# A Mamba-2 scan followed by hash-routed experts: the scan's decays split into a factor per step, its units halved, and expert weights held five at a time

## The chip, the cores and the metric

The kernel runs on one core of a Trainium2 chip. The metric is device time in microseconds (us) of one execution. TensorE (PE; PEld is its weight load), VectorE (DVE), ScalarE (ACT), GpSimd (POOL) and the queue engine SyncE (SP) each work through their own instructions in order and wait for each other on semaphores.

## The reference

First a state-space scan, for 4 batches x 8 heads over 768 steps, with head size D = 32 and state size N = 16. Each step has a decay a in 0.85 to 0.95. It is written in chunks of steps:

```python
cum = np.cumsum(la, axis=-1)                      # la = log(a), inside the chunk
L = np.exp(cum[:, :, :, None] - cum[:, :, None, :]) * causal
M = np.einsum('bhin,bhjn->bhij', Cc, Bc) * L
y = M @ xc + (Cc @ state) * np.exp(cum)[..., None]
state = exp(sum(la)) * state + sum_j B_j x_j * exp(cum[-1] - cum_j)
```

Then y, as 3072 tokens of 256 values, goes through one of 8 experts each, `relu(x @ w1[e]) @ w2[e]`, with e = token_id mod 8, w1 256 x 1024 and w2 1024 x 256, all in float32. The expert of the inputs with the most tokens has 403.

## The kernel before

**Scan.** 24 chunks of 128 steps (4 batches x 6), all 8 heads in one chunk. `prepare(b)` (L283) brings B and C of a batch into the layout states x steps: B and C are copied (`rows`, L293 and L295), transposed on PE (L299), written out as `bt` (L301) and `ce` (L307, L309: C with the odd or the even head of each pair set to zero), and B is transposed back and multiplied by its decays (`bs`, L315). `chunk` (L321) makes, for each half of the heads: `rl`, the log decays on a triangle (L334 on ACT, L336 on DVE); `seg`, their sums over steps, by a bf16 mask product (L338) and a float32 product of 512 columns (L340); `dl`, its exponential (L342); `gram`, C times B (L347, 32 rows of the array, 256 columns); `m`, their product (L349); and y (L353, 128 rows and columns, 32 columns streamed, one product per head). Then the carried state enters: `sp` (L360), its product with C (L364), the decays and the sum (L366, L369), a write to `y_tokens` in HBM (L370), and the new state from `bs` and x (L376) on DVE (L382).

**Routing.** `routing()` (L194, after chunk 1) turns token ids into a slot for each token, on DVE with three small matmuls; `slot_token` (L269) writes 128 slot numbers at a time to HBM from POOL; after the last one `idx_out` is loaded (L276, SP) and `idx_in` is made of it (L277, DVE). It holds the rows that each expert gathers.

**Experts.** Eight experts, up to 416 tokens each. Rows are gathered by POOL (L418), transposed (L441), multiplied (L454 up, L464 down, 128 x 128 weights and 416 columns), transposed back (L478) and scattered (L423). The loop for tokens over 416 (L513) has no round with these inputs. Weights of all 8 experts (16 MB) lie on chip; `load_w` (L102) issues them on ScalarE's queue, two loads of 1 MB per expert, from chunk 0 on, one expert every second chunk.

A scheduler orders the instructions of each engine from the program's text and its own costs, so the order on an engine is not the order of the text. Float32 matmuls are issued as two passes: the trace shows two MATMUL for each.

Of the kernel before, what the change touches and what calls it, by code (L numbers as in the profile page):

```python
# [20 lines left out]
def kernel(  # L21
# [97 lines left out]
    after = const.tile([P, P], F32)  # L119
    nc.vector.tensor_scalar(out=after, in0=upto, scalar1=-1.0, scalar2=1.0, op0=OP.mult, op1=OP.add)  # L120
    low = const.tile([P, P], BF16)
    nc.vector.tensor_scalar(out=low, in0=upto, scalar1=1000.0, scalar2=-1000.0, op0=OP.mult, op1=OP.add)  # L122

    gmask = const.tile([P, G, 2 * D], F32)
    nc.gpsimd.memset(gmask, 1.0)
    nc.gpsimd.affine_select(out=gmask, in_=gmask, pattern=[[-32, G], [0, 2 * D]], compare_op=OP.is_ge,
                            fill=0.0, base=0, channel_multiplier=1)
    nc.gpsimd.affine_select(out=gmask, in_=gmask, pattern=[[32, G], [0, 2 * D]], compare_op=OP.is_ge,
                            fill=0.0, base=31, channel_multiplier=-1)
# [13 lines left out]
    la_ps = ps_t.tile([P, R, BH], F32, name="tp")
    for c in range(R):
        nc.tensor.transpose(out=la_ps[:, c], in_=la[:, c * P:(c + 1) * P], identity=ident[0:BH, 0:BH])
    laT = const.tile([P, R, BH], F32)
    nc.vector.tensor_copy(out=laT, in_=la_ps)
    laf = laT.rearrange("p c j -> p (c j)")

    dec_ps = ps_t.tile([P, 2, R, BH], F32, name="tp")  # L150
    decf = dec_ps.rearrange("p i c j -> p i (c j)")
    nc.tensor.matmul(out=decf[:, 0], lhsT=upto, rhs=laf, start=True, stop=True)
    nc.tensor.matmul(out=decf[:, 1], lhsT=after, rhs=laf, start=True, stop=True)
# [11 lines left out]
    mhn = apre.tile([BH, H, NS], F32)
    nc.vector.tensor_copy(out=mhn, in_=mh.unsqueeze(2).to_broadcast([BH, H, NS]))
    totb = apre.tile([BH, NB, R], F32)
    nc.vector.tensor_tensor(out=totb, in0=tot.unsqueeze(1).to_broadcast([BH, NB, R]),
                            in1=mb.unsqueeze(2).to_broadcast([BH, NB, R]), op=OP.mult)
    pend_ps = ps_t.tile([P, NCH], F32, name="tp")  # L170
# [403 lines left out]
```

## Time and profile before

| | before |
|---|---|
| median of 3 runs | 471.72 us (470.3 to 471.89) |
| the profiled execution | 472.49 us, span 470.5, mean granted clock 0.862 |
| PE / PEld busy | 402.8 / 237.5 us |
| DVE / ACT / POOL busy | 150.8 / 94.8 / 93.3 us |
| moved by DMA | 33.28 MB, 57,868 packets |
| chain that ended last | PE 50%, issue 24%, DMA 16% |

Busy time is an engine's own; a busy PE is not PE at its peak, since its instructions' ends are modelled and overlap. The granted clock is 1.0 at 2.4 GHz and 0.5 at 1.2 GHz. In the timeline, `x8` is eight instructions merged in one row; what such a row costs its engine is the distance to the start of the next row. The bracket at the end of a row is the idle time before it and what ended it.

### The profile page before, as it was taken

Reading aid. Unit: us, or ns where it says so; the run is one execution under the profiler, and the core shown is the slowest. Engines: PE = TensorE matmul, PEld = TensorE weight load, DVE = VectorE, ACT = ScalarE, POOL = GpSimd, SP = SyncE. Lnnn points to the kernel's source line nnn. Section 1 sums busy time; section 2 is a strip of 40 time slices with the busy share of each in tenths; the row PEclk is TensorE's granted clock in tenths of the full one; section 3 lists DMA queues with packets and bytes.
Section 4 is the critical chain, followed back from the end, with each engine's and each line's share of the span. In section 5 each row is a group of like instructions: output and inputs, shape, how many; then the busy total and the mean of one; then the engine's idle time right before and its main releaser. Section 6 shows DMA issues by size and latency. Waiting matters only on the chain.

```text
span 470.5 us, 4814 instructions
## 1 busy us (share of the span) xinstructions
PE 402.8 (86%) x1689; PEld 237.5 (50%) x1690; DVE 150.8 (32%) x401; ACT 94.8 (20%) x217; POOL 93.3 (20%) x108
## 2 busy tenths in 40 slices
PE   0689988960699999999983999999999999999960
PEld 0347564620455666666661555555555555555530
DVE  2354853200223655765631121212121212122120
ACT  2151231120012344333320102011111111111110
POOL 1100174420000000000005430505050512020221
PEclk9996995555555899999995899999999999999985
DMA  8966729875233322210002110202020100000000
GB/s 296 230 199 201 225 31 134 124 98 110 23 111 114 111 48 45 46 34 25 23 22 66 55 33 3 66 4 68 3 66 6 55 15 33 0 35 0 26 32 13
DMA packets 57868, 33.28 MB, mean 71 GB/s; under 512 B 42799, under 2 KB 54089, under 8 KB 57844
## 3 DMA queue, kind: packets, MB, share of 16 engines
q10 hardware_dynamic: 10496, 16.78, 13.6%
q1 hardware_dynamic: 43764, 9.62, 10.4%
q0 software_dynamic: 3584, 6.57, 4.5%
q8 instruction: 14, 0.23, 0.2%
q14 instruction: 10, 0.08, 0.1%
HBM read 26.63 MB, written 6.59 MB: 71 GB/s over the span
## 4 chain that ended last, share of the span: by engine, by line
PE 50%; issue 24%; DMA 16%; POOL 5%; DVE 2%; ACT 1%; SPq 0%; POOLq 0%; DVEq 0%
PE h_ps L454 12%; PE o_ps L464 11%; PE y_ps L353 7%; PE seg L340 7%; DMA slot_tokens<-token,slot_i 5%; PE gram L347 5%; DMA out_dram<-o_sb,idx_out 4%; DMA bc<-in_C_dram 4%; POOL slot_tokens L270 2%; PE seg L338 2%; POOL out_dram L423 2%; PE y_ps L364 2%; DMA idx_out<-slot_tokens 2%; PE xt_ps L441 1%; PE tp L376 1%
## 5 line engine op out<-in xcount | busy, mean ns | idle before, releaser
L464 PE MATMUL o_ps<-hT,w_sb 128*128 128x416 f32 x256 | 102.1, 518 | 0.0
L454 PE MATMUL h_ps<-xT,w_sb 128*128 128x416 f32 x256 | 101.7, 522 | 0.3 <-DVE xT L442 0.3
L353 PEld LDWEIGHTS y_ps<-x_t,m 128*128 128x128 f32 x384 | 60.3, 231 | 21.6 <-issue 10.1
L464 PEld LDWEIGHTS o_ps<-hT,w_sb 128*128 128x128 f32 x256 | 47.5, 190 | 40.1 <-issue 36.3
L454 PEld LDWEIGHTS h_ps<-xT,w_sb 128*128 128x128 f32 x256 | 47.1, 194 | 32.2 <-issue 30.6
L340 PE MATMUL seg<-rl,after 128*128 128x512 f32 x96 | 62.0, 733 | 0.4 <-ACT rl L334 0.4
L353 PE MATMUL y_ps<-x_t,m 128*128 128x32 f32 x384 | 59.2, 303 | 0.9 <-DVE m L349 0.9
L418 POOL DMA_INDIRECT xg<-y_tokens,idx_in x32 | 32.0, 1001 | 122.1 <-issue 92.0
L342 ACT ACTIVATE dl<-seg 128x512 f32<-128x512 f32 x48 | 28.5, 599 | 128.5 <-PE seg L340 118.1
L423 POOL DMA_INDIRECT out_dram<-o_sb,idx_out x32 | 31.3, 977 | 114.1 <-ACT o_sb L481 95.8
L347 PE MATMUL gram<-ce,bt 32*128 32x256 f32 x192 | 48.0, 492 | 0.0
L448 DVE TENSOR_SCALAR hT<-h_ps 128x416 f32<-128x416 f32 x32 | 18.9, 592 | 74.4 <-PE h_ps L454 74.4
L349 DVE TENSOR_TENSOR m<-gram,dl 128x512 f32<-128x512 f32 x48 | 32.8, 687 | 28.5 <-PE gram L347 20.9
L446 ACT ACTIVATE hT<-h_ps 128x416 f32<-128x416 f32 x32 | 16.5, 517 | 99.9 <-PE h_ps L454 81.4
L442 DVE COPY xT<-xt_ps 128x256 f32<-128x256 f32 (+1 forms) x32 | 12.0, 375 | 70.8 <-PE xt_ps L441 70.0
L270 POOL DMA_INDIRECT slot_tokens<-token,slot_i x24 | 23.9, 996 | 48.2 <-DVE slot_i L259 28.2
L334 ACT ACTIVATE rl<-upto,laT 128x128 f32<-128x128 f32 x96 | 31.8, 390 | 0.0
L338 PE MATMUL seg<-low,ident 128*128 128x512 bf16 x48 | 20.9, 448 | 12.3 <-DVE low L122 10.9
L347 PEld LDWEIGHTS gram<-ce,bt 32*128 32x128 f32 x192 | 20.1, 211 | 19.8 <-issue 16.0
L336 DVE TENSOR_SCALAR rl<-upto,laT 128x128 f32<-128x128 f32 x96 | 23.7, 284 | 16.8 <-PE seg L340 13.2
L376 PE MATMUL tp<-x_t,bs 128*32 128x64 f32 x160 | 8.1, 260 | 20.0 <-DVE s_new L382 20.0
L340 PEld LDWEIGHTS seg<-rl,after 128*128 128x128 f32 x96 | 19.8, 230 | 5.4 <-issue 2.6
(109 smaller groups left out, 216.3 us busy)
## 6 DMA issues: line engine op xcount, KB each, us to landing
w_sb<-in_moe_w_dram ACTq DMA_DIRECT2D x16, 1024.0 KB
x_t<-in_x_dram SPq DMA_DIRECT2D x24, 128.0 KB
y_tokens<-y_sb SPq DMA_DIRECT2D x24, 128.0 KB
bc<-in_B_dram SPq DMA_DIRECT2D x4, 384.0 KB
bc<-in_C_dram SPq DMA_DIRECT2D x4, 384.0 KB
xg<-y_tokens,idx_in POOLq DMA_INDIRECT x32
out_dram<-o_sb,idx_out POOLq DMA_INDIRECT x32
slot_tokens<-token,slot_i POOLq DMA_INDIRECT x24
```

What stands on the lines that cost most here:

```text
L270: st = nc.gpsimd.indirect_dma_start(out=slot_dram[:, None], out_offset=bass.IndirectOffsetOnAxis(ap=slot_i[:, c:c + 1], axis=0), in_=token ...
L334: nc.scalar.activation(rl[:, k], upto, AF.Copy, scale=w)
L338: nc.tensor.matmul(out=seg, lhsT=ident16, rhs=low.unsqueeze(1).to_broadcast([P, HH, P]), start=True, stop=False)
L340: nc.tensor.matmul(out=seg, lhsT=after, rhs=rl, start=False, stop=True)
L342: nc.scalar.activation(dl, seg, AF.Exp)
L347: nc.tensor.matmul(out=gram[:, k, 0:2 * P], lhsT=bt[r, t], rhs=ce[r, :, t], start=True, stop=True)
L349: nc.vector.tensor_tensor(out=m.rearrange("p (k e) i -> p k (e i)", k=2), in0=gram[:, :, 0:2 * P], in1=dl.rearrange("p (k e) i -> p k (e i ...
L353: nc.tensor.matmul(out=y_ps[:, 0, h0 + k], lhsT=m[:, k], rhs=x_t[:, h0 + k], start=True, stop=True)
L418: nc.gpsimd.indirect_dma_start(out=dst, out_offset=None, in_=y_dram[:], in_offset=bass.IndirectOffsetOnAxis(ap=idx, axis=0), bounds_check= ...
L423: st = nc.gpsimd.indirect_dma_start(out=out[:], out_offset=bass.IndirectOffsetOnAxis(ap=idx, axis=0), in_=src, in_offset=None, bounds_chec ...
L454: nc.tensor.matmul(out=hp, lhsT=w1_sb[:, c:c + P], rhs=xT[e][:, i], start=(i == 0), stop=(i == DP - 1))
L464: nc.tensor.matmul(out=oP[e][:, j, 0:CAP], lhsT=w2_sb[:, c:c + P], rhs=h, start=(f == 0), stop=(f == FP - 1))
```

## The change

- **Decays.** exp(cum_i - cum_j) is split into a factor of step i and one of step j, both taken from the middle of a unit (`rel`, `fac`). They are multiplied into C and B when these are copied (`rows`, now both on DVE); `rl`, `seg`, `dl` and their products go, and `m` is gram times a 0/1 triangle.
- **Units of 64 steps.** A chunk is still 128 steps, as two units that lie on different halves of the array: gram on 32 x 64 tiles, the state's product and y on 64 x 64. Products across the two units are no longer made, so `m` has half the elements.
- **States.** `prepare` makes all 11 states of a batch: 24 products into `tp`, then for each unit on DVE `v`, the running state, and `up`, its head-masked copy times the step's decay. `chunk` multiplies `up` by a third copy of C (`ce[:, 2]`) into the free part of gram's banks; ScalarE copies that out (`z_sb`), and DVE adds it to y.
- **Weights.** Five buffers of w1 and w2. Loads are issued on SP, experts 0 to 4 in the scan, 5 to 7 when an expert has freed its buffer. The overflow loop loads its own weights.
- **Order.** `routing()` comes before `prepare(0)`; `slot_token` once per chunk. B and C have two buffers, x has 14 (before: 1 and 6).

```diff
+    NWB = 5
...
+    HL = P // 2
+    NU = S // HL
+    Q = P // BH
+    SQ = S // Q
+    UQ = SQ // HL
+    PQ = P // Q
...
-    ps_seg = pool(a_ctx, "ps_seg", 2, space=PSUM)
+    ps_t = pool(a_ctx, "ps_t", 2, space=PSUM)
     ps_g = pool(a_ctx, "ps_g", 2, space=PSUM)
-    ps_y = pool(a_ctx, "ps_y", 1, space=PSUM)
-    ps_t = pool(a_ctx, "ps_t", 1, space=PSUM)
-    a_t = apre.tile([BH, S], F32)
-    nc.sync.dma_start(out=a_t, in_=a.rearrange("b h s -> (b h) s"))
+    ps_y = pool(a_ctx, "ps_y", 2, space=PSUM)
+    a_t = apre.tile([P, SQ], F32)
...
+        t = aload.tile([P, 2, H, R * NS], F32, name="bc", bufs=2)
...
+        t = aload.tile([P, H, D], F32, name="x_t", bufs=14)
...
     load_bc(0)
...
+    for gc in range(R):
+        load_x(gc)
+    load_bc(1)
...
     def load_w(e):
...
+        w1s[e] = wpool.tile([P, DP, F], F32, name="w1", bufs=NWB)
+        nc.sync.dma_start(out=w1s[e], in_=moe_w1[e].rearrange("(k p) f -> p k f", p=P))
+        w2s[e] = wpool.tile([P, FP, DM], F32, name="w2", bufs=NWB)
+        nc.sync.dma_start(out=w2s[e], in_=moe_w2[e].rearrange("(k p) d -> p k d", p=P))
...
+    cum = apre.tile([P, UQ, HL], F32)
+    nc.vector.tensor_tensor_scan(out=cum.rearrange("p u t -> p (u t)"), data0=turn0.rearrange("p u t -> p (u t)"),
+                                 data1=a_t, initial=0.0, op0=OP.mult, op1=OP.add)
+    mid = cum[:, :, HL // 2 - 1:HL // 2]
+    rel = apre.tile([P, UQ, HL], F32)
+    nc.vector.tensor_tensor(out=rel, in0=cum, in1=mid.to_broadcast([P, UQ, HL]), op=OP.subtract)
+    fac = apre.tile([P, 2, SQ], F32)
+    relf = rel.rearrange("p u t -> p (u t)")
+    nc.scalar.activation(fac[:, 0], relf, AF.Exp, scale=-1.0)
+    nc.scalar.activation(fac[:, 1], relf, AF.Exp)
...
     def prepare(b):
         bt = abat.tile([P, S], F32, name="bt")
...
+        ce = abat.tile([P, 3, S], F32, name="ce")
+        bs = abat.tile([P, R, P], F32, name="bs", bufs=1)
         for i in range(2):
             rows = abat.tile([P, R, P], F32, name="rows", bufs=2)
...
+            nc.vector.tensor_tensor(
+                out=rows.rearrange("p r (h n) -> p r h n", h=H),
+                in0=bcs[b][:, i].rearrange("p h (r n) -> p r h n", r=R),
+                in1=dec[:, i, :, b * H:(b + 1) * H].unsqueeze(3).to_broadcast([P, R, H, NS]), op=OP.mult)
             for r0 in (0, R2):
                 tp = ps_t.tile([P, R2, P], F32, name="tp")
                 for r in range(R2):
                     nc.tensor.transpose(out=tp[:, r], in_=rows[:, r0 + r], identity=ident)
+                view = lambda o: o.rearrange("q (p r) -> q r p", r=R)[:, r0:r0 + R2]
                 if i == 0:
...
+                    nc.scalar.activation(view(bt), tp, AF.Copy)
                     continue
...
+                nc.scalar.activation(view(ce[:, 0]), tp, AF.Copy, scale=par[:, 0:1])
+                nc.vector.tensor_scalar(out=view(ce[:, 1]), in0=tp, scalar1=par[:, 1:2], scalar2=None, op0=OP.mult)
+                nc.scalar.activation(view(ce[:, 2]), tp, AF.Copy)
...
+            nc.scalar.activation(bs[:, c0:c0 + R2], tp, AF.Copy)
+        up = abat.tile([P, NU, G, D], F32, name="up")
+        nc.gpsimd.memset(up[:, 0], 0.0)
+        v = None
+        for c0 in (0, R2):
+            d_ps = [ps_t.tile([P, R2, P], F32, name="tp") for _ in range(2)]
+            for c in range(c0, c0 + R2):
+                for q in range(2):
+                    for u in range(2):
+                        nc.tensor.matmul(
+                            out=d_ps[u][q * HL:(q + 1) * HL, c - c0], lhsT=bs[u * HL:(u + 1) * HL, c, q * HL:(q + 1) * HL],
+                            rhs=xs[b * R + c][u * HL:(u + 1) * HL, q * G:(q + 1) * G].rearrange("p h d -> p (h d)"),
+                            start=True, stop=True)
+            for c in range(c0, c0 + R2):
+                for u in range(2):
+                    k = 2 * c + u
+                    if k == NU - 1:
+                        continue
+                    new = awork.tile([P, P], F32, name="v", bufs=4)
+                    if v is None:
+                        nc.vector.tensor_copy(out=new, in_=d_ps[u][:, c - c0])
+                    else:
+                        nc.vector.scalar_tensor_tensor(out=new, in0=v, scalar=step[:, b, k:k + 1],
+                                                       in1=d_ps[u][:, c - c0], op0=OP.mult, op1=OP.add)
+                    v = new
+                    nc.vector.scalar_tensor_tensor(out=up[:, k + 1].rearrange("p g d -> p (g d)"), in0=v,
+                                                   scalar=step[:, b, k + 1:k + 2],
+                                                   in1=own.rearrange("p g d -> p (g d)"), op0=OP.mult, op1=OP.mult)
+        bts[b], ces[b], ups[b] = bt, ce, up
...
+    def chunk(gc):
         b, c = divmod(gc, R)
...
+        bt, ce, up, x_t = bts[b], ces[b], ups[b], xs.pop(gc)
+        y_ps = ps_y.tile([P, 512], F32, name="y_ps")
+        z_sb = awork.tile([P, 2, P], F32, name="z_sb", bufs=3)
+        ms, gs = [], []
         for q in range(2):
...
+            gram = ps_g.tile([P, 2, 512], F32, name="gram")
             for k in range(2):
...
+                r = slice(32 * (2 * q + k), 32 * (2 * q + k) + 32)
+                for u in range(2):
+                    t = slice(c * P + u * HL, c * P + (u + 1) * HL)
+                    nc.tensor.matmul(out=gram[u * HL:(u + 1) * HL, k, 0:P], lhsT=bt[r, t], rhs=ce[r, 0:2, t],
+                                     start=True, stop=True)
+            m = awork.tile([P, G, HL], F32, name="m", bufs=4)
+            nc.vector.tensor_tensor(out=m.rearrange("p (k e) i -> p k (e i)", k=2), in0=gram[:, :, 0:P],
+                                    in1=causal.rearrange("p (k e) i -> p k (e i)", k=2), op=OP.mult)
+            ms.append(m)
+            gs.append(gram)
+        for q in range(2):
+            rq = slice(q * HL, (q + 1) * HL)
+            for u in range(2):
+                t = slice(c * P + u * HL, c * P + (u + 1) * HL)
+                nc.tensor.matmul(out=gs[q][u * HL:(u + 1) * HL, 0, P:2 * P], lhsT=ce[rq, 2, t],
+                                 rhs=up[rq, 2 * c + u].rearrange("p g d -> p (g d)"), start=True, stop=True)
+            nc.scalar.activation(z_sb[:, q], gs[q][:, 0, P:2 * P], AF.Copy)
+        for q in range(2):
+            for k in range(G):
+                for u in range(2):
+                    w = slice(u * HL, (u + 1) * HL)
+                    h = q * G + k
+                    nc.tensor.matmul(out=y_ps[w, h * D:(h + 1) * D], lhsT=ms[q][w, k], rhs=x_t[w, h],
+                                     start=True, stop=True)
+        y_sb = awork.tile([P, DM], F32, name="y_sb", bufs=3)
+        nc.vector.tensor_tensor(out=y_sb, in0=y_ps[:, 0:DM], in1=z_sb.rearrange("p q d -> p (q d)"), op=OP.add)
+        nc.sync.dma_start(out=y_dram[gc * P:(gc + 1) * P, :], in_=y_sb)
...
+    routing()
     prepare(0)
...
+    nw = 0
     for gc in range(NCH):
         b, c = divmod(gc, R)
...
         if c == 0 and b + 1 < NB:
+            for i in range(R):
+                load_x((b + 1) * R + i)
+        if c == 0 and 0 < b < NB - 1:
             load_bc(b + 1)
...
+        chunk(gc)
+        slot_token(gc)
+        if gc >= R and gc % 3 == 0 and nw < NWB:
+            load_w(nw)
+            nw += 1
+        if c == R2 and b + 1 < NB:
             prepare(b + 1)
+    while nw < NWB:
+        load_w(nw)
+        nw += 1
...
+            if e + NWB < E:
+                load_w(e + NWB)
```

The scheduler turns this into the following rows. On PE, near the end of the scan of the kernel before (`seg`, `gram` and `y_ps` as above; `tp` is the state's product; one row per product, not per pass):

```order
L347 MATMUL gram<-ce,bt 128x256 x2
L376 MATMUL tp<-x_t,bs 32x64 x4
L338 LDWEIGHTS ident_110
L338 MATMUL seg<-low,ident_110 128x512
L340 MATMUL seg<-rl,after 128x512
L353 MATMUL y_ps<-x_t,m 128x32 x4
L364 MATMUL y_ps<-sp,ce 128x4x32 x2
L347 MATMUL gram<-ce,bt 128x256 x2
L338 LDWEIGHTS ident_110
```

and of the changed kernel at the same place (L369 is gram, L381 the state's product, L389 y):

```order
L369 MATMUL gram<-ce,bt 64x128 x8
L381 MATMUL gram<-up,ce 64x128 x2
L389 MATMUL y_ps<-x_t,m 64x32 x6
L381 MATMUL gram<-up,ce 64x128 x2
L389 MATMUL y_ps<-x_t,m 64x32 x10
L369 MATMUL gram<-ce,bt 64x128 x8
L381 MATMUL gram<-up,ce 64x128 x2
L389 MATMUL y_ps<-x_t,m 64x32 x6
```

The 512-column rows are gone; a chunk is 8 gram, 2 x 2 state and 16 y products, and gram of the next chunk stands behind y of this one.

On DVE, around `idx_in` in the kernel before (`s_new` is the carried state, m and y_sb as above):

```order
L380 COPY s_new<-tp 128x64
L336 TENSOR_SCALAR rl<-upto,laT 128x128 x2
L360 TENSOR_TENSOR sp<-s_new,gmask 128x256
L277 TENSOR_SCALAR idx_in<-idx_out 128x53
L336 TENSOR_SCALAR rl<-upto,laT 128x128 x2
L382 SCALAR_TENSOR_TENSOR s_new<-s_new,pend,tp 128x64
L360 TENSOR_TENSOR sp<-s_new,gmask 128x256
L349 TENSOR_TENSOR m<-gram,dl 128x512 x2
```

and in the changed kernel (`v` and `up` are the carry of the last batch):

```order
L348 SCALAR_TENSOR_TENSOR v<-v,step,tp 128x128
L372 TENSOR_TENSOR m<-gram,causal 128x256
L351 SCALAR_TENSOR_TENSOR up<-v,step,own 128x128
L348 SCALAR_TENSOR_TENSOR v<-v,step,tp 128x128
L292 TENSOR_SCALAR idx_in<-idx_out 128x53
L351 SCALAR_TENSOR_TENSOR up<-v,step,own 128x128
L348 SCALAR_TENSOR_TENSOR v<-v,step,tp 128x128
L351 SCALAR_TENSOR_TENSOR up<-v,step,own 128x128
L348 SCALAR_TENSOR_TENSOR v<-v,step,tp 128x128
L392 TENSOR_TENSOR y_sb<-y_ps,z_sb 128x256
```

`idx_out` is awaited in the middle of a batch in both; behind it stood L336 and m of the next chunk, now the rest of the last batch's carry.

On SP of the changed kernel, the last weight loads of the scan (`w_1351`, `w_1589` and `w_1591` are weights of experts 3 and 4):

```order
L393 DMA y_tokens<-y_sb 128x256
L111 DMA w_1351<-in_moe_w_dram 128x8x256
L393 DMA y_tokens<-y_sb 128x256 x2
L109 DMA w_1589<-in_moe_w_dram 128x2x1024
L393 DMA y_tokens<-y_sb 128x256 x2
L111 DMA w_1591<-in_moe_w_dram 128x8x256
L291 DMA idx_out<-slot_tokens 128x53x1
L393 DMA y_tokens<-y_sb 128x256
```

`idx_out` has moved behind the weights of the fifth expert and 16 of the 24 y writes; before, six y writes stood ahead of it and no weights were on this queue.

## Rows read from the trace of the kernel before

**Rows 1.** Timeline from the last output of the scan to the first expert

```profile
246.76 0.42 DVE L369 TENSOR_TENSOR y_sb<-y_ps,y_sb 128x256 f32<-128x256 f32 x1
...
250.09 1.07 POOL L418 DMA_INDIRECT xg<-y_tokens,idx_in  x1 [89.22 <-issue]
...
257.64 6.51 PE L454 MATMUL h_ps<-xT,w_sb 128*128 128x416 f32 x12 [0.32 <-DVE xT L442]
```

**Rows 2.** Three stretches of the scan: busy time by engine, granted clock, DMA share, GB/s

```profile
core 0: us, PE busy (x) PEld busy (x) DVE busy (x) ACT busy (x) POOL busy (x), PEclk, DMA share, GB/s
16.00:72.00 56.00, 48.92 (x248) 31.06 (x248) 31.78 (x100) 17.42 (x42) 12.01 (x12) 0.87 0.61 170
72.00:156.00 84.00, 63.39 (x213) 37.27 (x213) 19.59 (x57) 11.56 (x30) 13.55 (x14) 0.50 0.59 101
156.00:244.00 88.00, 86.72 (x571) 56.90 (x569) 54.23 (x145) 35.61 (x86) 0.91 (x1) 1.00 0.18 46
```

**Rows 3.** Timeline around the longest gap: start us, us, engine, line, what [idle before]

```profile
112.82 0.37 SPq L276 DMA_DIRECT2D idx_out<-slot_tokens  x1
...
120.71 0.19 DVE L277 TENSOR_SCALAR idx_in<-idx_out 128x53 int32<-128x53 int32 x1 [29.96 <-DMA idx_out<-slot_tokens]
...
121.53 0.43 PE L376 MATMUL tp<-x_t,bs 128*32 128x64 f32 x6 [20.03 <-DVE s_new L382]
```

**Rows 4.** Timeline of PE at half clock, two stretches, and three transposes

```profile
58.58 0.84 PE L299 MATMUL tp<-ident,rows 128*128 128x128 f32 x3
...
89.01 0.44 PE L376 MATMUL tp<-x_t,bs 128*32 128x64 f32 x8
89.39 1.03 PE L338 MATMUL seg<-low,ident 128*128 128x512 bf16 x2
...
126.61 1.75 PE L353 MATMUL y_ps<-x_t,m 128*128 128x32 f32 x8
128.17 1.20 PE L364 MATMUL y_ps<-sp,ce 128*128 128x128 f32 x4
129.30 1.23 PE L347 MATMUL gram<-ce,bt 32*128 32x256 f32 x4
130.46 2.08 PE L340 MATMUL seg<-rl,after 128*128 128x512 f32 x2
```

**Rows 5.** Timeline of PE at full clock, one stretch of a chunk

```profile
218.23 0.70 PE L347 MATMUL gram<-ce,bt 32*128 32x256 f32 x4
218.87 0.32 PE L376 MATMUL tp<-x_t,bs 128*32 128x64 f32 x8
...
220.20 0.97 PE L353 MATMUL y_ps<-x_t,m 128*128 128x32 f32 x8
221.01 0.69 PE L364 MATMUL y_ps<-sp,ce 128*128 128x128 f32 x4
221.63 0.70 PE L347 MATMUL gram<-ce,bt 32*128 32x256 f32 x4
```

**Rows 6.** Groups by shape: count | busy us, mean ns of one | idle before

```profile
L349 DVE TENSOR_TENSOR m<-gram,dl 128x512 f32<-128x512 f32 x48 | 32.8, 687 | 28.5 <-PE gram L347 20.9 <-ACT rl L334 7.4
...
L309 DVE TENSOR_SCALAR ce<-tp,par 128x384 f32<-128x384 f32 x8 | 7.2, 904 | 6.0 <-ACT ce L307 5.7 <-issue 0.3
...
L366 DVE TENSOR_TENSOR y_sb<-y_ps,dec 128x256 f32<-128x256 f32 x20 | 8.5, 423 | 26.7 <-PE y_ps L364 26.7
...
L315 DVE TENSOR_TENSOR bs<-tp,dec 128x128 f32<-128x128 f32 x24 | 5.5, 283 | 3.9 <-PE tp L313 2.3 <-remote 1.5
```

**Rows 7.** Timeline of the start: B lands, first outputs of the scan

```profile
9.87 0.56 DVE L293 COPY rows<-bc 128x768 f32<-128x768 f32 x1 [6.14 <-DMA bc<-in_B_dram]
...
37.12 0.38 ACT L357 ACTIVATE y_sb<-y_ps 128x256 f32<-128x256 f32 x1 [3.64 <-PE y_ps L353]
```

**Rows 8.** DMA queues of the page: packets, MB, share of 16 engines over the span

```profile
q10 hardware_dynamic: 10496, 16.78, 13.6%
q1 hardware_dynamic: 43764, 9.62, 10.4%
```

More of the change, by code (lines that the diff above doesn't have):

```diff
@@ L45 @@
     FP = F // P
-    WS = DP * F
+    NWB = 5
     CAP = 416
@@ L118 @@
                             fill=0.0, base=0, channel_multiplier=-1)
[L119 to L129, printed above, removed]
+    causal = const.tile([P, G, HL], F32)
+    for u in range(2):
+        nc.vector.tensor_copy(out=causal[u * HL:(u + 1) * HL],
+                              in_=upto[0:HL, 0:HL].unsqueeze(1).to_broadcast([HL, G, HL]))
+    turn0 = const.tile([P, UQ, HL], F32)
+    nc.vector.memset(turn0, 1.0)
+    nc.vector.memset(turn0[:, :, 0:1], 0.0)
     hm = const.tile([P, G, 2], F32)
@@ L137 @@
     nc.vector.tensor_reduce(out=par, in_=hm.rearrange("p g e -> p e g"), axis=AX.X, op=OP.add)
+    own = const.tile([P, G, D], F32)
+    hq = const.tile([P, G], F32)
+    hm8 = hm.rearrange("p g e -> p (g e)")
+    nc.vector.tensor_tensor(out=hq, in0=hm8[:, 0:G], in1=hm8[:, G:2 * G], op=OP.add)
+    nc.vector.tensor_copy(out=own, in_=hq.unsqueeze(2).to_broadcast([P, G, D]))
+    idv = ident.rearrange("p (b h q) -> p b h q", b=NB, h=H)
+    selq = const.tile([P, Q, BH], F32)
+    nc.vector.tensor_copy(out=selq, in_=ident.rearrange("p (j q) -> p q j", q=Q))
@@ L143 @@
[L143 to L153, printed above, removed]
@@ L165 @@
[L165 to L170, printed above, removed]
-    nc.tensor.matmul(out=pend_ps, lhsT=mhn.rearrange("p h n -> p (h n)"),
-                     rhs=totb.rearrange("p b c -> p (b c)"), start=True, stop=True)
@@ new lines @@
+    fac = apre.tile([P, 2, SQ], F32)
+    relf = rel.rearrange("p u t -> p (u t)")
+    nc.scalar.activation(fac[:, 0], relf, AF.Exp, scale=-1.0)
+    nc.scalar.activation(fac[:, 1], relf, AF.Exp)
+    fac_ps = ps_t.tile([P, 2, R, BH], F32, name="tp")
+    for i in range(2):
+        for r in range(R):
+            for q in range(Q):
+                nc.tensor.matmul(out=fac_ps[q * PQ:(q + 1) * PQ, i, r],
+                                 lhsT=fac[:, i].rearrange("p (t r) -> p r t", r=R)[:, r], rhs=selq[:, q],
+                                 start=True, stop=True)
@@ new lines @@
+    dec = const.tile([P, 2, R, BH], F32)
+    nc.vector.tensor_copy(out=dec, in_=fac_ps)
+    ends = apre.tile([P, 2, UQ], F32)
+    nc.vector.tensor_copy(out=ends[:, 0], in_=mid.rearrange("p u o -> p (u o)"))
+    nc.vector.tensor_copy(out=ends[:, 1], in_=rel[:, :, HL - 1])
+    endb = apre.tile([P, 2, NB * Q, UQ], F32)
+    for i in range(2):
+        nc.vector.tensor_tensor(out=endb[:, i], in0=ends[:, i].unsqueeze(1).to_broadcast([P, NB * Q, UQ]),
+                                in1=mbq.rearrange("p b q -> p (b q)").unsqueeze(2).to_broadcast([P, NB * Q, UQ]),
+                                op=OP.mult)
@@ new lines @@
+    end_ps = ps_t.tile([P, 2, NB, NU], F32, name="tp")
+    nc.tensor.matmul(out=end_ps.rearrange("p i b u -> p (i b u)"), lhsT=mhn.rearrange("p h n -> p (h n)"),
+                     rhs=endb.rearrange("p i c u -> p (i c u)"), start=True, stop=True)
+    step = const.tile([P, NB, NU], F32)
+    nc.vector.tensor_copy(out=step, in_=end_ps[:, 0])
+    nc.vector.tensor_tensor(out=step[:, :, 1:], in0=step[:, :, 1:], in1=end_ps[:, 1, :, 0:NU - 1], op=OP.add)
+    nc.scalar.activation(step, step, AF.Exp)
@@ L370, in chunk @@
-        nc.sync.dma_start(out=y_dram[gc * P:(gc + 1) * P, :], in_=y_sb.rearrange("p h d -> p (h d)"))
-        if c == R - 1:
-            return None
-        d_ps = ps_t.tile([P, 2 * D], F32, name="tp")
-        for g in range(G):
-            nc.tensor.matmul(out=d_ps[32 * g:32 * g + 32, :], lhsT=bs[:, c, 32 * g:32 * g + 32],
-                             rhs=x_t[:, 2 * g:2 * g + 2].rearrange("p h d -> p (h d)"), start=True, stop=True)
-        s_new = awork.tile([P, 2 * D], F32, name="s_new")
@@ L540 @@
         for f in range(FP):
[L541 removed]
+            nc.tensor.matmul(out=op, lhsT=hlT[:, f], rhs=w2l[:, f],
                              start=(f == 0), stop=(f == FP - 1))
```

146 lines of the change are left out of this document (25 added, 121 removed).

## The prediction

> **What bounds the kernel now.** I read the windows by stage first, then the timeline of the stage that changes, then the groups by shape for prices. The run has two parts that do not overlap. The scan ends with the last y_sb at 247.2 us, and the first expert's matmul starts at 257.64 [rows 1]; from there to the end of the span, 470.5, it is 213 us of experts. The change leaves the experts' arithmetic as it is, so the question is when the scan ends.
>
> The windows cut the scan in three [rows 2]. From 72 to 156 TensorE was granted half its clock (0.50, 1.2 GHz of 2.4), from 156 to 244 all of it. In the last stretch PE is busy 86.7 of 88 us: there the scan is bound by PE. In the middle one PE is busy 63.4 of 84 us, and the missing 20 are one gap: VectorE stands still for 30 us in front of idx_in until idx_out, issued at 112.82, has landed; it goes on at 120.71, and PE, which waits for s_new behind it, at 121.53 after 20.03 us idle [rows 3]. So the scan loses its time to three things: matmuls in number, half clock, and one wait of VectorE for a small load.
>
> **PE in a chunk.** What goes: the products `seg` (twice a chunk, 512 columns in two passes, 2.08 us at half clock [rows 4]) with their bf16 mask matmul, the y products with 128-column weights, the ScalarE exponentials and the `rl` copies. What comes is 8 gram matmuls (32 rows by 64 columns of the array, 128 columns streamed), 4 for the carried state (64 by 64, 128 streamed) and 16 for y (64 by 64, 32 streamed), two passes each.
>
> The price of a pass comes from gram now. At full clock its four instructions (two matmuls on two row strips, 256 columns) hold PE from 218.23 to 218.87, 0.64 us [rows 5]; that is three times 0.213, so the second pass of one matmul runs beside the first pass of the next, and n matmuls on different strips cost n+1 passes. At half clock the same four take 129.30 to 130.46, 1.16 us [rows 4], or 0.39 per pass. For 128 columns that is 0.107 and 0.19 us. The y products now take 0.81/8 = 0.10 us per instruction at full clock (220.20 to 221.01) and 1.56/8 = 0.195 at half (126.61 to 128.17) [rows 4, 5]; they stream only 32 columns, so it is the 128-column weights that cost, and 64-column weights cost half, 0.051 and 0.098.
>
> A chunk after the change, at half clock: gram 2 x 5 x 0.19 = 1.9, state 2 x 3 x 0.19 = 1.15, y 17 x 0.098 = 1.7 (its two units lie on different rows and columns, so I let them overlap as gram's strips do): **4.7 us**. At full clock: 1.07 + 0.64 + 0.86 = **2.6 us**. The trace has no 64 by 64 tile, so both ends: below, the 8 small instructions of L376 on four column strips hold PE for 0.38 us at half clock (89.01 to 89.39 [rows 4]), 0.048 each, and 56 instructions cost 2.7 us; above, nothing overlaps and nothing is halved: 24 x 0.28 (L364, 1.13 us for four, 128.17 to 129.30 [rows 4]) + 32 x 0.195 = 13 us. I take 4.7, since gram's row is the nearest kind.
>
> **PE in a prepare.** 18 transposes at 0.84/3 = 0.28 us [rows 4] are 5.0; 24 matmuls for the states (two passes, 128 columns, four tiles) are 25 x 0.19 = 4.8. Three of the four prepares lie inside the scan: 29 us. PE also waits there for ScalarE and VectorE to free two PSUM buffers; I put 3 us per prepare, 9 in all (bounds 0 and, for six evictions of 0.90 us like L309 [rows 6], 5 each).
>
> **VectorE.** It gives up rl, sp and one half of m, and gets the carry: per batch 11 v and 11 up of 128 elements. A 128-element operation is 0.28 us, 256 elements 0.42, ce 0.90 [rows 6]. After the first m: 48 m and 24 y_sb x 0.42 = 30, 88 carry steps x 0.30 = 26, six ce 5, four `rows` x 0.95 = 4: 65 us, under PE's 142 at half clock. It hides there; were PE at full clock (78), it would be close.
>
> **The start.** Routing moves ahead of the first prepare, and VectorE does some 25 small operations (6 us) before the first chunk. In exchange no weight competes with B, C and x. B was used first at 9.87 and the first output came at 37.12 [rows 7]. Queue q1 moved 43,764 packets with 10.4% of 16 engines' 470.5 us, 49 us, 1.12 ns a packet [rows 8]; up to the second batch's C there are 10 loads of 1,024 packets, 11.5 us, so `rows` of batch 1, which VectorE reaches early, holds it until about 13. Then 11.5 us of routing, ce and carry: first m at **26 us**.
>
> **Queues.** The weights of five experts move from ScalarE's queue to SP's, behind the y writes; SP carries y, x, B, C, idx_out and weights in order. q10 took 13.6% of the span for 16 loads [rows 8], 4 us each. Ten weight loads (40 us) and q1's 49 us make 89, under a scan of 140 or more; y has three buffers. The other six loads start when an expert's weights come free, five experts (over 120 us) before use; hidden, and 8 us per expert if they were not. POOL loses a copy of rows; all 24 slot writes stand in one run behind slot_i. idx_in stays a wait of VectorE in the middle of a carry: idx_out now stands on SP behind the fifth expert's second load. The slots are long written then, so it waits for its own landing, 7.9 us now (112.82 to 120.71 [rows 3]), and up to 8 us of weights ahead of it, while VectorE has some 10 us of work before it. I charge **4 us** (0 to 16).
>
> **Clock.** Half clock held for 84 us with PE busy in all of it but the gap [rows 2]; full clock came in stretches with the 512-column products. The changed scan has none, and streams 32 or 128 columns on parts of the array. I take half clock for four fifths of PE's 142 us; the other fifth at full clock gives back 0.2 x 142 x 0.45 = 13.
>
> **Sum.** 26 + 24 x 4.7 (113) + 29 + 9 + 4 - 13 = **168 us** for the scan's end, 79 before 247.2. The way to the first expert (10.4 us) and the experts (213) stay. The profiled execution took 472.5 us (span 470.5), so 393; it is 0.8 above the median of the runs, 471.7: I say **392**. This case alone, with the chunk between 3.5 and 6 us: 365 to 425.
>
> **Rivals.**
> *Full clock.* PE needs 24 x 2.6, and 5.2 in each of three prepares (25 x 0.107, transposes at half their price), 78; with 26, 12 of waits and 4 the scan ends at 120, still above the DMA floor of 91: 345 us. For it: the last 88 us kept full clock although PE had gaps [rows 2]. Against it: the middle stretch kept half clock with heavier matmuls [rows 2]. Chance 0.28.
>
> *The y units do not overlap.* They write one PSUM bank from two row halves; gram's strips write two banks, so the trace cannot tell. Then y costs 32 x 0.098 = 3.1, 1.4 more per chunk, 35 in all: 427. Chance 0.06. The Trainium skill (TensorEngine Tiling (Array Packing), Gotcha 1: PSUM Pressure) says that different row tiles cannot access the same PSUM bank at once; by that rule the sum is 427 and not 392; no run here shows it yet.
>
> *A drain at each change of tile shape.* gram has 32-row, the rest 64-row tiles, the transposes the whole array, about four changes per chunk. At up to 0.44 us each (one small matmul's length [rows 4]) that is 42 us: 434. Against it: gram on 32 rows is followed by L376 on 32 columns 0.64 us later, exactly its three passes [rows 5]. Chance 0.05. The same page (Key Properties) says that changing the tiling mode, not just the tile, drains TensorE; by that rule 434; [rows 5] shows no such price.
>
> *The wait for idx_out returns in full.* 20 us instead of 4: 408. Chance 0.04.
>
> *Slower: the parts of the array do not overlap at all.* The place is PE in each chunk; the price is the 13 us above. The scan then ends at 26 + 312 + 3 x 18 + 13 = 405, the kernel near 630. It decides from (247 - 26 - 42)/24 = 7.5 us a chunk. Against it: gram's strips overlap at both clocks [rows 4, 5]. Chance 0.04. The forecast has the rest, 0.53.
>
> **Numbers.** 335 to 428 covers the forecast and full clock, with some 5 us below for its unknowns, and leaves out the slowest cases and their tails. About 0.5% is what a measurement of this kernel can tell from no change. Faster in all cases but the last, and that at a price far over: faster 0.95, same 0.01, slower 0.04.
>
> **What would show it.** Right: last y_sb near 168, clock at 0.5 in most of it, gram and y groups near 1.0 and 0.85 us per half chunk, VectorE idle over a third, a wait at idx_in of a few us. Wrong: clock 1.00 through the chunks; y instructions spaced by 0.1 us at half clock; PE idle before the state matmuls, which would mean that the carry on VectorE binds; an expert waiting for weights.

## The result and the profile after

The changed kernel takes 388.35 us (median of four runs, 386.07 to 389.92); the kernel before took 471.81 beside it (470.3 to 473.9). The ratio is 0.8225, 95% interval 0.8172 to 0.8278. Predicted were 392 us and a scan that ends at 168. The profiled execution took 386.07 us, its span 384.3.

The timeline of the changed kernel, the first m and the place where the scan meets the experts, in the columns of [rows 1] (start, duration, engine, line, operation, tiles, count, idle time before and its releaser):

```profile
24.75 0.41 DVE L372 TENSOR_TENSOR m<-gram,causal 128x256 f32<-128x256 f32 x1
...
161.39 0.42 DVE L392 TENSOR_TENSOR y_sb<-y_ps,z_sb 128x256 f32<-128x256 f32 x1 [2.43 <-ACT z_sb L383]
...
172.16 5.82 PE L464 MATMUL h_ps<-xT,w 128*128 128x416 f32 x12 [0.41 <-DVE xT L453]
```

The scan ends at 161.8, against 247.2 [rows 1]; the first expert begins 10.4 us later, as before, and the experts fill the rest, 212 us to 384.3. No expert waits for weights. Of the 86.2 us that the span lost, 85.4 lie in the scan. Its windows (columns as in [rows 2]):

```profile
16.00:24.00 8.00, 6.20 (x46) 3.98 (x46) 5.52 (x23) 2.53 (x5) 0.00 (x0) 0.62 1.24 176
24.00:72.00 48.00, 42.41 (x512) 33.55 (x514) 24.08 (x69) 12.04 (x26) 24.01 (x25) 0.50 0.88 101
72.00:88.00 16.00, 6.34 (x99) 4.85 (x96) 3.63 (x8) 2.28 (x6) 0.00 (x0) 0.50 0.85 150
88.00:162.00 74.00, 67.22 (x944) 55.23 (x944) 32.58 (x93) 16.50 (x43) 0.20 (x1) 0.50 0.42 119
```

Two things strike the eye. The granted clock is 0.50 from 18 us on, in all of the chunks and not in four fifths. And from 72 to 88 PE is busy for 6.3 of 16 us: a hole that the prediction does not have. One chunk near the end, on PE:

```profile
146.06 0.73 PE L369 MATMUL gram<-ce,bt 32*64 32x128 f32 x16
147.31 0.48 PE L381 MATMUL gram<-up,ce 64*64 64x128 f32 x2 [0.52 <-DVE m L372]
...
148.51 1.42 PE L389 MATMUL y_ps<-x_t,m 64*64 64x32 f32 x19
149.86 0.73 PE L369 MATMUL gram<-ce,bt 32*64 32x128 f32 x16
```

From gram to gram are 3.80 us: 0.73 for all 16 passes of gram, 0.52 in which PE stands because z (L381) writes the bank that VectorE reads for m, and 2.55 for z and y, which the scheduler wove together.

The hole, on VectorE and PE, and what SyncE's queue did meanwhile (SPq rows: start and duration of an issue):

```profile
75.98 0.42 DVE L392 TENSOR_TENSOR y_sb<-y_ps,z_sb 128x256 f32<-128x256 f32 x1 [6.75 <-DMA y_tokens<-y_sb]
...
85.45 0.96 DVE L306 TENSOR_TENSOR rows<-bc,dec 128x768 f32<-128x768 f32 x1 [8.39 <-DMA bc<-in_B_dram]
...
134.11 0.19 DVE L292 TENSOR_SCALAR idx_in<-idx_out 128x53 int32<-128x53 int32 x1 [0.61 <-DMA idx_out<-slot_tokens]
```
```profile
76.79 0.48 PE L381 MATMUL gram<-up,ce 64*64 64x128 f32 x2 [2.55 <-DVE m L372]
...
88.16 0.69 PE L324 MATMUL tp<-ident,bt 128*128 128x128 f32 x2 [7.27 <-ACT ce L320]
```
```profile
67.17 8.11 SPq L94 DMA_DIRECT2D x_t<-in_x_dram  x2
75.33 7.12 SPq L88 DMA_DIRECT2D bc<-in_B_dram  x1
82.54 0.99 SPq L393 DMA_DIRECT2D y_tokens<-y_sb  x1
```

A y write has not landed, then B of the third prepare is late: it was issued at 75.33 only, and its issue took 7.12 us. PE stands for 2.55 and 7.27 us behind them, 9.8 in all. In exchange the wait for idx_out, 20 us before [rows 3], is 0.61.

### The profile page after: what moved, and what is told of

It reads as the page before. It is cut to its first block, busy times and chain, and to the rows that moved or that the text cites. A ratio compares the mean times of both kernels' runs of the same rounds, so it can differ in the third digit from the quotient of the medians.

```text
span 384.3 us, 5938 instructions
## 1 busy us (share of the span) xinstructions
PE 328.4 (85%) x2351; PEld 212.1 (55%) x2351; DVE 117.4 (31%) x319; ACT 67.3 (18%) x142; POOL 89.2 (23%) x105
## 4 chain that ended last, share of the span: by engine, by line
PE 59%; issue 17%; DMA 9%; DVE 6%; POOL 3%; ACT 2%; SPq 0%; POOLq 0%; DVEq 0%
PE h_ps L464 15%; PE o_ps L473 14%; PE y_ps L389 9%; DMA out_dram<-o_sb,idx_out 5%; PE gram L381 5%; PE gram L369 5%; PE tp L335 4%; PE tp L313 3%; DMA bc<-in_B_dram 3%; POOL out_dram L434 2%; PE tp L324 2%; DVE m L372 1%; PE xt_ps L452 1%; PE ot_ps L490 1%; DVE y_sb L392 1%
## 5 line engine op out<-in xcount | busy, mean ns | idle before, releaser
L473 PE MATMUL o_ps<-hT,w 128*128 128x416 f32 x256 | 102.1, 518 | 0.0
L464 PE MATMUL h_ps<-xT,w 128*128 128x416 f32 x256 | 101.0, 519 | 0.4 <-DVE xT L453 0.4
L473 PEld LDWEIGHTS o_ps<-hT,w 128*128 128x128 f32 x256 | 47.5, 190 | 40.1 <-issue 36.3
L389 PE MATMUL y_ps<-x_t,m 64*64 64x32 f32 x768 | 65.6, 291 | 0.0
L464 PEld LDWEIGHTS h_ps<-xT,w 128*128 128x128 f32 x256 | 46.8, 193 | 31.9 <-issue 30.7
L389 PEld LDWEIGHTS y_ps<-x_t,m 64*64 64x64 f32 x768 | 61.5, 219 | 0.0
L381 PE MATMUL gram<-up,ce 64*64 64x128 f32 x192 | 33.2, 440 | 10.9 <-DVE m L372 10.6
L381 PEld LDWEIGHTS gram<-up,ce 64*64 64x64 f32 x192 | 16.1, 205 | 21.9 <-DVE m L372 12.2
L369 PE MATMUL gram<-ce,bt 32*64 32x128 f32 x384 | 27.0, 442 | 0.0
L392 DVE TENSOR_TENSOR y_sb<-y_ps,z_sb 128x256 f32<-128x256 f32 x24 | 10.2, 424 | 49.3 <-ACT z_sb L383 19.0
L335 PE MATMUL tp<-x_t,bs 64*64 64x128 f32 x192 | 20.0, 427 | 0.5 <-DVE v L348 0.5
L372 DVE TENSOR_TENSOR m<-gram,causal 128x256 f32<-128x256 f32 x48 | 19.0, 417 | 3.8 <-PE gram L369 2.6
```

The source lines that it names most:

```text
L335: nc.tensor.matmul(out=d_ps[u][q * HL:(q + 1) * HL, c - c0], lhsT=bs[u * HL:(u + 1) * HL, c, q * HL:(q + 1) * HL], rhs=xs[b * R + c][u * H ...
L369: nc.tensor.matmul(out=gram[u * HL:(u + 1) * HL, k, 0:P], lhsT=bt[r, t], rhs=ce[r, 0:2, t], start=True, stop=True)
L372: nc.vector.tensor_tensor(out=m.rearrange("p (k e) i -> p k (e i)", k=2), in0=gram[:, :, 0:P], in1=causal.rearrange("p (k e) i -> p k (e i ...
L381: nc.tensor.matmul(out=gs[q][u * HL:(u + 1) * HL, 0, P:2 * P], lhsT=ce[rq, 2, t], rhs=up[rq, 2 * c + u].rearrange("p g d -> p (g d)"), sta ...
L389: nc.tensor.matmul(out=y_ps[w, h * D:(h + 1) * D], lhsT=ms[q][w, k], rhs=x_t[w, h], start=True, stop=True)
L464: nc.tensor.matmul(out=hp, lhsT=w1s[e][:, i, f * P:(f + 1) * P], rhs=xT[e][:, i], start=(i == 0), stop=(i == DP - 1))
```

## The experiments

Who makes the hole? Candidates: the 1 MB weight loads on SyncE's queue, or the 24 writes of slot_tokens, which stand in one run on GpSimd's queue from 25 to 68 us. Their row in the page's DMA issues (count, median us to landing):

```profile
slot_tokens<-token,slot_i POOLq DMA_INDIRECT x24, 13.8
```

Four kernels came first.

**Weights on ScalarE's queue.** Each load tied by a one-column write from the y_sb after which it was issued:

```diff
-        nc.sync.dma_start(out=w1s[e], ...)
+        nc.scalar.activation(w1s[e][:, 0, 0:1], y_sb[:, 0:1], AF.Copy)
+        nc.scalar.dma_start(out=w1s[e], ...)
```

> The ten weight loads of the scan go from SyncE's queue to ScalarE's, each tied to the y_sb after which it was issued, so that none comes earlier. Theory A (SyncE's queue is in order and the 1 MB loads hold up the y writes, x and B behind them): the hole of PE around 73 to 88 us, some 10 us, goes, B of the third prepare lands before it is wanted, the scan ends near 152 and the kernel near 378 us. Theory B (the 16 DMA engines are full between 40 and 72 us, share 0.95 to 1.32, by whatever queue): the hole stays, the time stays within 385 to 391 us. A third way: ScalarE is itself held while it issues (up to 4.5 us for one load on SyncE now), z_sb is late, and some us come back.

401.86 us (401.05 to 404.07): slower, by something else. With the weights gone from SyncE's queue idx_out moved up in it, and idx_in up on VectorE:

```profile
81.37 0.19 DVE L295 TENSOR_SCALAR idx_in<-idx_out 128x53 int32<-128x53 int32 x1 [25.09 <-DMA idx_out<-slot_tokens]
```

That wait covers the place of the hole, so whether the hole goes with the weights the run does not tell. It does show the engines full without them: its first weight is issued at 94.55 us, and two windows of it read

```profile
40.00:48.00 8.00, 7.03 (x90) 5.73 (x91) 3.67 (x8) 3.53 (x7) 2.92 (x3) 1.00 1.27 75
48.00:56.00 8.00, 7.98 (x88) 5.81 (x87) 3.51 (x9) 4.08 (x8) 2.49 (x3) 1.00 0.94 91
```

a DMA share of 1.27 and 0.94 at 75 and 91 GB/s. The run also prices the wait for idx_out in full: VectorE stood for 25 us, and PE for 24.8, where the rival had 20.

**Slot writes spread over the chunks.**

```diff
     def slot_token(c, y_sb):
+        nc.vector.scalar_tensor_tensor(out=tokd[:, c:c + 1], in0=y_sb[:, 0:1], scalar=0.0, in1=token[:, c:c + 1], ...)
-            in_=token[:, c:c + 1], ...
+            in_=tokd[:, c:c + 1], ...
```

> The 24 slot writes no longer stand in one run from 25 to 68 us: each waits for the y_sb of a chunk (four in three chunks, the last with chunk 17), by an operation of VectorE of one column. The weights stay on SyncE's queue. Theory A (the order of SyncE's queue): no change, hole of some 10 us stays, 385 to 392 us. Theory B (the slot writes fill the DMA engines: share over 0.95 at 12 to 77 GB/s, 13.8 us to land): weights, y and B land earlier, the hole goes, near 378 us. idx_out comes late, so a wait of VectorE near the scan's end of up to 8 us may take some of it.

385.34 us (383.1 to 388.26). The weights are on SyncE's queue as before, the first four issued at 31.7, 45.2, 51.0 and 55.4 us (changed kernel: 32.2, 45.3, 55.8 and 60.0), and the hole is gone. The windows 40 to 88 us, of the changed kernel and of this one:

```profile
40.00:56.00 16.00, 15.81 (x191) 12.38 (x189) 7.19 (x14) 7.03 (x13) 5.89 (x6) 0.50 1.26 106
56.00:72.00 16.00, 14.06 (x186) 11.25 (x186) 8.56 (x28) 3.05 (x8) 8.00 (x9) 0.50 0.96 164
72.00:88.00 16.00, 6.34 (x99) 4.85 (x96) 3.63 (x8) 2.28 (x6) 0.00 (x0) 0.50 0.85 150
```
```profile
40.00:56.00 16.00, 15.05 (x206) 12.11 (x207) 8.36 (x22) 6.71 (x13) 3.09 (x4) 0.50 0.55 113
56.00:72.00 16.00, 14.46 (x198) 11.89 (x198) 7.90 (x28) 2.51 (x7) 3.90 (x5) 0.50 0.85 174
72.00:88.00 16.00, 13.70 (x176) 10.93 (x170) 7.11 (x18) 6.51 (x13) 3.88 (x4) 0.50 0.89 103
```

PE is busy for 13.7 us where it had 6.3, and the DMA engines carry about as much from 40 to 56 (113 GB/s, before 106) at a share of 0.55 in place of 1.26. The total hardly shows it: the ranges of the two kernels overlap, and in both profiled executions the scan ends near 161.8. The time came back as other waits, most of it one: idx_out came late, VectorE stood 5.61 us at idx_in and PE 6.0 behind it.

**No weights before chunk 17.** `if gc >= 17 and nw < NWB` in place of `gc >= R and gc % 3 == 0`.

> No weight is asked for before chunk 17 in the program; then all five experts' loads follow. Theory A and theory B with the weights as the load that fills the engines: the hole goes, the scan ends near 152, near 378 us, unless the first expert then waits for its weights (they need some 10 us after about 115 us, so no). If the slot writes alone fill the engines: the hole stays, 385 to 391 us.

388.16 us (385.58 to 390.04), no change, and the hole is there; VectorE waits for y writes:

```profile
79.19 0.42 DVE L392 TENSOR_TENSOR y_sb<-y_ps,z_sb 128x256 f32<-128x256 f32 x1 [6.79 <-DMA y_tokens<-y_sb]
...
88.25 0.42 DVE L392 TENSOR_TENSOR y_sb<-y_ps,z_sb 128x256 f32<-128x256 f32 x1 [7.16 <-DMA y_tokens<-y_sb]
```

But this is not a run without weights ahead of the hole. The edit moved the loads in the program's text, and the scheduler issued them early all the same, the first expert's two before the hole (the changed kernel has four loads there) and the next two in it, at 79.72 and 86.43:

```profile
54.64 3.66 SPq L109 DMA_DIRECT2D w<-in_moe_w_dram  x1
...
59.79 5.98 SPq L111 DMA_DIRECT2D w<-in_moe_w_dram  x1
```

So w_late does not decide, and theory A falls by slot_spread: with the weights on the same queue at nearly the same times, and only the slot writes spread, the hole is gone. The weights by themselves do not make it. Whether the slot writes would make it with no weight at all is not shown; that the engines are as full without any, w_act shows.

**z in the bank of y.** The carried products go to columns 256 to 511 of y's bank: `out=y_ps[u * HL:(u + 1) * HL, 256 + q * P:256 + (q + 1) * P]`.

> The carried-state products z go into unused columns of the chunk's y bank and no longer into the bank of gram, which VectorE reads for m. Theory: z waits for m only by that place; it then fills the 0.52 us in which PE now stands in each chunk: 24 x 0.52 = 12 us less where the chunk is bound by PE, some 377 us. Rival: z of both row halves in one bank no longer overlap, so z costs 1.1 in place of 0.64 us and the gain shrinks to 0 to 2 us. Rival: y waits for m instead and PE stands as long: no change.

404.84 us (403.14 to 408.39), 16 slower where 11 less were expected. z no longer waits for m. The end of the scan on PE, and the group of gram in the page of the changed kernel and in this one's (busy us, mean ns):

```profile
166.62 1.12 PE L381 MATMUL y_ps<-up,ce 64*64 64x128 f32 x8
167.67 0.68 PE L369 MATMUL gram<-ce,bt 32*64 32x128 f32 x2
168.28 0.69 PE L381 MATMUL y_ps<-up,ce 64*64 64x128 f32 x4
168.90 0.70 PE L369 MATMUL gram<-ce,bt 32*64 32x128 f32 x8
169.53 1.92 PE L389 MATMUL y_ps<-x_t,m 64*64 64x32 f32 x32
```
```profile
L369 PE MATMUL gram<-ce,bt 32*64 32x128 f32 x384 | 27.0, 442 | 0.0
```
```profile
L369 PE MATMUL gram<-ce,bt 32*64 32x128 f32 x384 | 40.5, 442 | 0.0
```

With z in another tile the scheduler chose another order. It put gram's passes in small groups between products of other shapes, and each group costs about 0.62 us, whether it has 2 passes (167.67 to 168.28) or 8 (168.90 to 169.53). The same 384 passes take 13.5 us more. That is only half of it: PE is busy for 357.3 us, before 328.4. In the changed kernel z was woven with y, and most of it ran in y's time; here it stands in groups of its own (168.28 to 168.90), and z and y together hold PE for some 13 us more, added up from row to row over the scan. z's eight passes, both row halves in one bank, also take longer, 1.12 us against 0.71 in two banks in the changed kernel:

```profile
70.81 0.71 PE L381 MATMUL gram<-up,ce 64*64 64x128 f32 x8
```

**The two units of y in two banks, and in one as the control.** Both have one y buffer of two banks and two y_sb operations of 64 partitions; the index of the bank is the unit or 0.

```diff
-        y_ps = ps_y.tile([P, 512], F32, name="y_ps")
+        y_ps = ps_y.tile([P, 2, 512], F32, name="y_ps")
-            nc.tensor.matmul(out=y_ps[w, h * D:(h + 1) * D], ...)
+            nc.tensor.matmul(out=y_ps[w, u, h * D:(h + 1) * D], ...)
```

> The y products of the two units of a chunk write two PSUM banks instead of one (one y buffer of two banks in place of two of one; y_sb is made by two operations of VectorE of 64 partitions). Theory (two units that write one bank do not run side by side: 32 passes x 0.052 us = 1.65 us, which is what y takes now): y falls to about 0.9 us, the chunk from 3.79 to about 3.1, 24 x 0.7 = 17 us less, near 371 us, somewhat more if the second y_sb operation delays m. Rival (y is bound by something else, such as the weight load of each pass, whatever the bank): the chunk stays at 3.8 and the time at 386 to 395 us.

> The control of the run before: the same single y buffer and the same two y_sb operations, but both units write one bank. Both theories: the chunk stays at 3.8 us or a little above (the second y_sb operation, about 0.3 us, may delay m), 386 to 396 us.

402.97 us (402.48 to 404.43) in two banks and 404.51 (404.0 to 405.41) in one. A chunk is 4.08 us in both, and y's rows are the same, first of two banks, then of one:

```profile
154.27 1.85 PE L389 MATMUL y_ps<-x_t,m 64*64 64x32 f32 x27
```
```profile
155.34 1.85 PE L389 MATMUL y_ps<-x_t,m 64*64 64x32 f32 x27
```

So the bank does not bound y. The 16 us over the changed kernel stood elsewhere: between 28 and 66 us VectorE and ScalarE waited for a releaser that the trace calls remote, for up to 15 us at a time.

**Added products of the whole array.** Three or eight per chunk:

```diff
+        for _ in range(8):
+            nc.tensor.matmul(out=y_ps[:, 256:512], lhsT=ident16, rhs=wide16, start=True, stop=True)
```

> Three bf16 products on the whole array, 256 columns each, are added to every chunk; their result is not read. Theory (the clock is at half because the products of the scan cover parts of the array only): the clock rises, three transposes take 0.55 us in place of 0.83 to 0.90, the chunk falls to about 3 us, some 370 us. Rival (the clock stays at half): each costs 0.21 us and the change to the whole array and back 0.2 us each, 1.0 us less up to 0.5 that falls in PE's wait for m, times 24: 400 to 413 us.

> The same with eight such products a chunk. Clock rises: chunk of about 3.4 us, some 380 us. Clock stays: 1.7 us and two changes of 0.2 more a chunk, less up to 0.5, times 24: 425 to 440 us. The difference of eight and three, 5 products, prices one without the changes around it.

412.43 us (408.32 to 415.94) and 406.22 (392.01 to 416.74). With three the granted clock was 0.50 from 88 us on; with eight, in the profiled execution (416.74), it went up and down, and in a stretch at full clock gram's 16 passes took 0.47 us and 28 of y 1.06. Both had the remote waits too, so their times say little.

**The control, the slot writes in six groups of four, and two of the above on top.** The tie is made once for four slots, after chunks 1, 4, ... 16; idx_out and idx_in go to GpSimd's queue, ahead of the gathers that need them:

```diff
+        if gc % 3 == 1 and gc < 18:
+            tie(y_sb, gc // 3 * 4, gc // 3 * 4 + 4)
-            nc.sync.dma_start(out=idx_out, ...)
-            nc.vector.tensor_scalar(out=idx_in, ...)
+            nc.gpsimd.dma_start(out=idx_out, ...)
+            nc.gpsimd.tensor_scalar(out=idx_in, ...)
```

> The changed kernel once more, as the control on the same chip as the three that follow. Expected: 386 to 390 us as in its own runs. If the 16 us by which the four runs of one y buffer and of the added products came out slower belonged to their chip and not to the kernels, it takes some 400 here.

> The slot writes go out four at a time, after chunks 1, 4, 7, 10, 13 and 16 (one tie operation of VectorE for four), and idx_out and idx_in move to GpSimd's queue, so that neither VectorE nor SyncE waits for them. Theory (the run of 24 slot writes is what makes the hole, and with them spread only the wait for idx_out was left): no wait of VectorE over 3 us in the chunks, last y_sb near 153, 376 to 380 us. Rival (the weights on SyncE's queue make the hole as well): 384 to 388.

> The run before with one y buffer and two y_sb operations. Theory (the 16 us of the earlier run with one y buffer were loads of instructions and small transfers that stood behind the slot writes): the waits in 28 to 66 us that the trace calls remote go, and what is left is 0.3 us a chunk, 7 us over the run before: 383 to 388. Rival (they come from the one y buffer itself): 16 us over the run before, near 394.

> The slot writes spread, and eight bf16 products of the whole array in each chunk. Theory (the clock is at half because the products of the scan lie on parts of the array): without the early holes full clock holds through most of the scan, gram of a chunk takes 0.47 and y 1.06 us, the chunk some 3.4, 368 to 380 us. Rival (the clock goes on changing between its two levels): 385 to 410 us.

The control took 390.15 us (388.88 to 392.27): the chip is not the cause. **slot_ends took 378.13** (376.72 to 378.56), 12 us less than the control beside it and faster than both kernels; to the kernel before its ratio is 0.8178 (0.8145 to 0.8212), that of the control 0.8449 (0.8393 to 0.8505). The kernel before ranged from 461.7 to 482.3 us beside them, so the two are best compared with each other. The hole, 13.6 us of PE in the control, is down to 3.1. Last y_sb at 158.6, not 153: some waits stay:

```profile
75.81 0.42 DVE L397 TENSOR_TENSOR y_sb<-y_ps,z_sb 128x256 f32<-128x256 f32 x1 [6.86 <-issue]
...
121.78 0.42 DVE L397 TENSOR_TENSOR y_sb<-y_ps,z_sb 128x256 f32<-128x256 f32 x1 [4.49 <-DMA y_tokens<-y_sb]
```

Nor are the 12 us all the slot writes'. The control's scan ends at 165.9 and this one's at 159.0, 6.8 us sooner. The other 5.6 lie behind the last scatter, in the control and here:

```profile
377.49 0.88 POOL L434 DMA_INDIRECT out_dram<-o_sb,idx_out  x1 [0.30 <-issue]
```
```profile
370.84 0.88 POOL L443 DMA_INDIRECT out_dram<-o_sb,idx_out  x1 [0.30 <-issue]
```

From the end of these rows to the end of the span (388.6 and 376.3) are 10.2 and 4.6 us. The end is short in the three kernels with idx_out and idx_in on GpSimd's queue and 10.2 to 10.7 in all others, so it came with that second change; how, no run shows. Without it the time would have been near 384 (an estimate, 378.1 + 5.6), at the rival's price: that the total met its forecast of 376 to 380 is luck.

With one y buffer on top it took 378.88 (378.45 to 385.99), not 394, and the scan ends at 159.2, as without: the 16 us go when the slot writes are spread. The remote waits of VectorE and ScalarE, with one y buffer, first the run of slot writes and then the groups of four (total us, times, longest):

```profile
DVE v L348 <- remote: 5.3, 1, 5.3
DVE m L372 <- remote: 0.5, 1, 0.5
ACT z_sb L383 <- remote: 18.7, 2, 15.0
ACT bs L325 <- remote: 5.7, 1, 5.7
ACT ce L318 <- remote: 4.4, 1, 4.4
```
```profile
DVE v L353 <- remote: 1.7, 1, 1.7
```

Its chunk is still 4.08 us at the end, against 3.79 without; why that does not show in the total I did not settle. With eight added products it took 397.11 (391.91 to 403.52): in the profiled execution (403.52) the granted clock went between 0.50 and 1.00 until 104 us and stayed at 0.50 behind it, where each group of eight costs 1.8 us. Holding the clock up this way does not pay.

## Why the prediction was right

The sum was 168 for the scan's end and 161.8 came out. Step by step:

- **The start.** First m at 24.75, predicted 26: right, 1.3 less.
- **A chunk at half clock.** 3.80 in place of 4.7, 22 us over 24 chunks. The step that failed is gram at n+1 passes, 1.9 us. The eight tiles run side by side: a group of gram costs 0.62 to 0.66 us whether it has 2 passes or 16. z and y were 2.85 and measured 2.55, right. What was missing is PE's 0.52 us for m.
- **Prepares.** 38 us predicted with their waits; the scan's 137 us from the first m, less 91 for chunks and 9.8 for the hole, leave 36. This is a remainder, so it makes the sum below close by itself. Counted from row to row on PE instead, the prepares' products take 30 us (29 predicted) and those of the chunks 87, with the hole 9.8 and some 10 of other waits. Right.
- **Queues.** Half right: no expert waits for a weight, and idx_in waited 0.61 us, not 4. "All 24 slot writes stand in one run" was in the text, but no price was put on it: 10 us of hole, which go in slot_spread and, but for 3, in slot_ends.
- **The clock.** The credit of 13 us was wrong. The granted clock fell to 0.50 at 18 us, after PE had stood 2.51 us for ce, and rose at 175, three us into the experts' products on the whole array.

So: -1.3 - 22 - 2 - 3.4 + 13 + 9.8 = -6, which is the scan's end to half a us. The mechanism held: the scan is bound by PE at half clock, without the 512-column products. That the total came within 4 us is luck: a term taken too high (gram) met a credit that did not come (the clock) and a term at nothing (the slot writes).

The rivals. *Full clock* did not come. *The y units*: two banks change nothing, so 427 falls, though whether the units run side by side at 0.10 us a pass or one after the other at 0.05 stays open. The Trainium skill (TensorEngine Tiling (Array Packing), Gotcha 1: PSUM Pressure) says that row tiles cannot use one bank at once; z agrees (1.12 us in one bank, 0.71 in two), y does not show it. *The drain*: the 42 us did not come, but the mechanism is there, smaller. Transposes in groups between other shapes, in the changed kernel:

```profile
42.00 0.47 PE L313 MATMUL tp<-ident,rows 128*128 128x128 f32 x1
42.40 0.48 PE L381 MATMUL gram<-up,ce 64*64 64x128 f32 x2
...
92.36 0.90 PE L324 MATMUL tp<-ident,bt 128*128 128x128 f32 x3
93.19 2.19 PE L335 MATMUL tp<-x_t,bs 64*64 64x128 f32 x24
```

One takes 0.40 to the next shape, three 0.83: 0.21 each, and some 0.2 on top of each group. The changed kernel's chunk has two such changes, an estimated 0.4 us, not four of 0.44. The prediction read 0.64 us of gram [rows 5] as three passes and no change; it may hold one, and no run separates the two. The Trainium skill (TensorEngine Tiling (Array Packing), Key Properties) says that a change of the tiling mode drains TensorE; the rows fit that, at about 0.2 us. z_bank shows what small groups cost when a scheduler scatters them. *No overlap* (slower) fell with gram's row. *idx_out in full* came in w_act alone.

## What to carry to other kernels

Price every transfer that moves, small ones most of all: with 24 writes of 4-byte elements in one run, y and B came late and PE stood for 10 us; spread, they left no such hole, with the weights in the queue where they were. Keep products of one shape together: a group of gram costs 0.62 us with 2 passes and 0.66 with 16, and an edit that removes a wait of 0.52 us and lets a scheduler scatter the groups can cost more than the wait. Read in the trace whether an edit did what it was meant to: in w_late the loads still came early, and in slot_ends nearly half of the gain lay at another place.

## What the runs showed of the hardware

- **The slot writes.** From 48 to 56 us of the changed kernel the DMA engines stood at a share of 1.32 and moved 59 GB/s:

```profile
48.00:56.00 8.00, 7.93 (x89) 5.87 (x87) 3.81 (x8) 3.36 (x6) 1.94 (x2) 0.50 1.32 59
```

- **Remote waits.** VectorE and ScalarE stood for up to 17 us at a releaser that the trace calls remote, while the slot writes ran. That they waited for loads of instructions is my reading: the trace of busy3 has packets of the instruction queues in two such stretches, 27 to 40 and 50 to 63 us. But the changed kernel has such packets too, from 40 to 50 and 60 to 70 us, and no such wait. It was not tested by itself.
- **The record of the clock can be wrong.** w_late, w_act, z_bank, slot_ends and the control show 1.00 throughout the scan, but the first 12 matmuls of the experts take 5.83 us in w_late and 5.82 in the changed kernel, at a recorded 0.50 for the first three of these us, and the chunk is 3.80 in both. I went by durations. The Trainium skill (TensorE: Matmul & The Clock Gate, Seeing it yourself) warns that the clock's events in a trace can be unreliable; these runs agree.
